# Eight instead of six buffers for the q and k chunks of a fused attention and star-ReLU kernel

## The chip, the cores and the metric

The kernel runs on one core of one Trainium2 chip. The metric is the device time of one execution in microseconds (us), the median of several. TensorE is called PE below (PEld is its weight load), VectorE DVE, ScalarE ACT, GpSimd POOL, SyncE SP. "L566" is line 566 of the program; in experiments that add lines the same statement has a number up to eight higher.

## The reference, cut to what matters

```python
def _attn_ref(q, k, v, tau):                 # each (4, 6080, 256), float32
    qn = q / (np.linalg.norm(q, axis=1, keepdims=True) + 1e-06)
    kn = k / (np.linalg.norm(k, axis=1, keepdims=True) + 1e-06)
    s = kn.transpose(0, 2, 1) @ qn / tau     # 256 x 256 for each batch
    a = softmax(s)                           # cut: max, exp, sum
    return v @ a

def _moe_ref(x, w_in, w_out, s, b):          # x: 24320 x 256, w_in: 256 x 2048
    r = np.maximum(x @ w_in, 0.0)
    return (s * (r * r) + b) @ w_out
```

For each of the four batches the kernel needs the whole of q and k, summed into one 256 x 256 matrix (the "Gram" matrix), before it can start on that batch's rows. It does so for a batch while PE works on the rows of the one before. Only the first batch has nothing to hide behind.

## The kernel before

q and k arrive in chunks of 512 rows (13 chunks for the first batch, 12 for each later one). One buffer holds one chunk of both in fp16, 4 KiB a partition. The four fp32 pieces of w_out have the same size and take buffers of the same pool.

```python
    qk_pool = pool("qk_pool", 6)
    # ... (cut)
        def load(self, c):
            at, np_, jc = self.chunks[c]
            t = qk_pool.tile([P, 2, JC, C], FP16, tag="qk", name="qk")
            # ... (cut: the first two chunks of batch 0 take another way)
                    po(nc.gpsimd.dma_start(out=t[:np_, i, :jc, :], in_=rows))
    # ... (cut) after the first batch's chunks:
    for i in range(NPIECE):                                     # 4 pieces
        w32 = qk_pool.tile([P, 4, C], FP32, tag="qk", name="w32")
        po(nc.gpsimd.dma_start(out=w32, in_=w_out_rows[:, ts(i, 4), :]))
        w_pieces.append(w32)
```

`po` keeps the instructions of an engine in program order. So POOL issues the loads of q, k and v one after the other, and a load whose buffer isn't free holds up all behind it. A tile's buffer is chosen when the program is built: a free one, or the one that is given back next.

The work of the later batches is spread over numbered program steps. What matters here is the second batch (batch 1): chunk c is loaded 16 steps ahead of its use, its four pairs of Gram matmuls (L142) follow, and its squares for the norms come on ACT (k) and DVE (q, L162):

```python
            for j in range(JC):
                at_step(w0 + span * (c * JC + j) / n, lambda gr=gr, c=c, j=j: gr.mm(c, j))

            def norm_step(gr=gr, c=c, sc=sc):
                ops = gr.norm_ops(c)          # square of k, square of q, two folds
                for i, f in enumerate(ops):
                    at_step(int(sc) + 2 + 1 + i * 3, f)
```

The pieces of w_out are read by casts and sums at steps 7 to 44; the last reader of piece 1 comes at step 38 (L470), of piece 4 at step 44. The third chunk is asked for at step 24.

## Time and profile before

| | before |
|---|---|
| median of the first three runs | 730.93 us (729.64 to 731.26) |
| span of the profiled run | 727.9 us (its time: 729.62 us) |
| PE busy, first 40 us | 25.58 us |
| PE busy, 76 to 721 us | 644.39 of 645 us |
| waits of PE from 40 to 722 us | 3.2 us, of them 2.0 in one piece |

The table says that PE is the bound from 40 us on, and that reading the first batch is a stage of its own, limited by the transfers. The rows that carry it are in the prediction.

### The profile page before, as it was taken

Reading aid. Unit: us, or ns where it says so; the run is one execution under the profiler, and the core shown is the slowest. Engines: PE = TensorE matmul, PEld = TensorE weight load, DVE = VectorE, ACT = ScalarE, POOL = GpSimd, SP = SyncE. Lnnn points to the kernel's source line nnn. Section 1 sums busy time; section 2 is a strip of 40 time slices with the busy share of each in tenths; the row PEclk is TensorE's granted clock in tenths of the full one; section 3 lists DMA queues with packets and bytes.
Section 4 is the critical chain, followed back from the end, with each engine's and each line's share of the span. In section 5 each row is a group of like instructions: output and inputs, shape, how many; then the busy total and the mean of one; then the engine's idle time right before and its main releaser. Section 6 shows DMA issues by size and latency. Waiting matters only on the chain.

```text
span 727.9 us, 17843 instructions
## 1 busy us (share of the span) xinstructions
PE 705.5 (97%) x7618; PEld 509.7 (70%) x7618; DVE 623.9 (86%) x873; ACT 541.6 (74%) x582; POOL 82.4 (11%) x158
## 2 busy tenths in 40 slices
PE   4799899999999999999999999999999999999997
PEld 3556677776777777777677777777668777777776
DVE  4779899988888989898788989998888888888886
ACT  4489777787777777788777777778777777777872
POOL 4520420001121110001110210000000000000000
PEclk9999999999999999999999999999999999999999
DMA  9995995236497654333767585323333333321201
GB/s 235 209 258 69 209 207 109 61 88 128 92 142 161 128 96 99 88 73 66 141 124 137 119 145 130 71 62 72 84 74 77 88 75 73 96 59 47 78 30 74
DMA packets 81600, 79.57 MB, mean 109 GB/s; under 512 B 55696, under 2 KB 56528, under 8 KB 81520
## 3 DMA queue, kind: packets, MB, share of 16 engines
q0 software_dynamic: 21472, 39.46, 31.9%
q1 hardware_dynamic: 59616, 37.64, 19.9%
q8 instruction: 60, 0.98, 0.6%
q10 hardware_dynamic: 432, 1.31, 0.5%
q14 instruction: 20, 0.16, 0.1%
HBM read 78.91 MB, written 24.90 MB: 143 GB/s over the span
## 4 chain that ended last, share of the span: by engine, by line
PE 89%; DMA 5%; ACT 3%; DVE 2%; issue 1%; POOL 0%; ACTq 0%; POOLq 0%; DVEq 0%
PE h_ps L566 43%; PE o_ps L710 38%; PE s_ps L142 4%; DMA qk<-in_q_dram 3%; PE wa_ps L278 2%; ACT r L576 1%; DMA raw<-in_q_dram 1%; PE o_ps L614 1%; ACT g L587 1%; ACT sq L165 0%; ACT L222 0%; DVE f L178 0%; PE t_ps L241 0%; DVE o_sb L594 0%; DVE S L638 0%
## 5 line engine op out<-in xcount | busy, mean ns | idle before, releaser
L576 ACT ACTIVATE r<-h_ps 128x1024 f16<-128x1024 f32 (+1 forms) x384 | 387.8, 1013 | 154.3 <-PE h_ps L566 152.7
L566 PE MATMUL h_ps<-vT,wa 128*128 128x512 f16 (+7 forms) x1632 | 451.9, 364 | 0.6 <-ACT r L576 0.4
L710 PEld LDWEIGHTS <-S 128*128 128x128 f16 x2944 | 198.1, 98 | 86.3 <-issue 1.5
L710 PEld LDWEIGHTS <-g 128*128 128x128 f16 x2208 | 155.0, 98 | 74.1
L589 DVE TENSOR_TENSOR g<-r 128x2048 f16<-128x2048 f16 (+2 forms) x154 | 176.3, 1145 | 17.7 <-ACT r L576 17.3
L710 PE MATMUL o_ps<-T,S 128*128 128x128 f16 x2208 | 183.7, 219 | 0.9 <-ACT nrm L222 0.4
L566 PEld LDWEIGHTS <-wa 128*128 128x128 f16 x1632 | 136.2, 98 | 21.6 <-issue 1.0
L710 PE MATMUL o_ps<-w_out,g 128*128 128x128 f16 x1472 | 134.2, 219 | 0.0
L594 DVE SCALAR_TENSOR_TENSOR o_sb<-o_ps,s_out,u 128x256 f32<-128x256 f32 x138 | 66.4, 481 | 52.8 <-PE o_ps L710 50.8
L587 ACT ACTIVATE g<-r 128x1024 f16<-128x1024 f16 x93 | 97.9, 1053 | 0.0
L142 PE MATMUL s_ps<-qk 128*128 128x256 f16 (+1 forms) x384 | 70.6, 285 | 15.6 <-ACT qk L133 7.0
L325 POOL DMA_DIRECT2D v<-in_v_dram x48 | 25.7, 536 | 506.3 <-DMA vT<-v 346.4
L594 DVE SCALAR_TENSOR_TENSOR u<-o_ps,s_out,rowconst 128x256 f32<-128x256 f32 x138 | 65.9, 478 | 3.6 <-PE o_ps L710 2.4
L710 PE MATMUL o_ps<-w_out,S 128*128 128x128 f16 x736 | 63.4, 219 | 0.0
L710 PE MATMUL o_ps<-N,g 128*128 128x128 f16 x736 | 63.4, 219 | 0.0
L165 ACT ACTIVATE sq<-qk 128x1024 f16<-128x1024 f16 (+3 forms) x49 | 50.4, 1033 | 10.7 <-DMA qk<-in_k_dram 7.5
L638 DVE TENSOR_TENSOR S<-S,g 128x2048 f16<-128x2048 f16 (+1 forms) x47 | 56.4, 1201 | 1.3
L636 DVE TENSOR_TENSOR S<-g 128x2048 f16<-128x2048 f16 (+1 forms) x47 | 56.0, 1192 | 0.0
L642 DVE TENSOR_TENSOR S<-g,S 128x2048 f16<-128x2048 f16 x46 | 55.9, 1215 | 0.0
L640 DVE TENSOR_TENSOR S<-g 128x2048 f16<-128x2048 f16 x46 | 55.8, 1214 | 0.0
L142 PEld LDWEIGHTS <-qk 128*128 128x128 f16 (+1 forms) x384 | 33.1, 102 | 21.7 <-DVE qk L132 9.1
L162 DVE TENSOR_TENSOR sq<-qk 128x1024 f16<-128x1024 f16 (+3 forms) x49 | 33.0, 673 | 2.8 <-DMA qk<-in_q_dram 2.8
(68 smaller groups left out, 281.6 us busy)
## 6 DMA issues: line engine op xcount, KB each, us to landing
out_dram<-o_sb SPq DMA_DIRECT2D x46, 512.0 KB, 3.0
v<-in_v_dram POOLq DMA_DIRECT2D x47, 256.0 KB, 3.9
qk<-in_k_dram POOLq DMA_DIRECT2D x42, 256.0 KB, 6.8
qk<-in_q_dram POOLq DMA_DIRECT2D x42, 256.0 KB, 7.6
vT<-v SPq DMA_TRANSPOSE x182, 2.8
w<-in_moe_w_out_dram POOLq DMA_DIRECT2D x4, 512.0 KB, 12.0
raw<-in_q_dram ACTq DMA_DIRECT2D x2, 512.0 KB, 6.6
raw<-in_k_dram SPq DMA_DIRECT2D x2, 512.0 KB, 7.0
```

What stands on the lines that cost most here:

```text
L142: po(nc.tensor.matmul(self.s_ps[:, ch, :], kc[:np_, j, ts(ch, P)], qc[:np_, j, :], start=(c == 0 and j == 0 and ch == 0), stop=(c == len(s ...
L165: po(nc.scalar.activation(out=st["sq"][:np_, 1, js, :], in_=kc[:np_, js, :], func=AF.Square))
L566: po(nc.tensor.matmul(dst, wa[:, ci, ts(m, P)], src, start=(ci == 0), stop=(ci == CH - 1), skip_group_check=True))
L576: po(nc.scalar.activation(out=r16[:, :, i % 2, :n], in_=h_tiles.pop((g, i))[:, :, :n], func=AF.Relu))
L587: po(nc.scalar.activation(out=dst, in_=src, func=AF.Square))
L589: po(nc.vector.tensor_mul(dst, src, src))
L594: po(nc.vector.scalar_tensor_tensor(out=dst, in0=src, scalar=s_out, op0=ALU.mult, in1=add, op1=ALU.add))
L636: po(nc.vector.tensor_add(T[1], A21, A22))
L638: po(nc.vector.tensor_sub(T[2], T[1], A11))
L640: po(nc.vector.tensor_sub(T[3], A11, A21))
L642: po(nc.vector.tensor_sub(T[4], A12, T[2]))
L710: po(nc.tensor.matmul(st[name][:, j, :], a()[:, i, ts(j, P)], w[:, i, :], start=first, stop=last, skip_group_check=True))
```

## The change

It is to keep the second batch's first chunks from waiting for buffers that hold w_out.

```diff
-    qk_pool = pool("qk_pool", 6)
+    qk_pool = pool("qk_pool", 8)
```

No instruction is added, removed or moved: the programs of the two kernels are the same on every engine, but for addresses and waits.

## The prediction

> **What bounds the kernel now.** I read the page first, then the table of waits for TensorE (PE) alone, then the order of work on GpSimd and PE around the one wait that matters, then DMA use in 2 us steps.
>
> ```profile
> span 727.9 us, 17843 instructions
> PE 705.5 (97%) x7618; PEld 509.7 (70%) x7618; DVE 623.9 (86%) x873; ACT 541.6 (74%) x582; POOL 82.4 (11%) x158
> PE 89%; DMA 5%; ACT 3%; DVE 2%; issue 1%; POOL 0%; ACTq 0%; POOLq 0%; DVEq 0%
> ```
>
> PE is busy for 97% of the span and holds 89% of the chain that ended last. So a buffer can be worth only the time in which PE stands still for it. Busy time of PE by stretches gives where it stands: 25.58 of the first 40.00 us (the first batch's q and k are being read), 32.16 of 40 to 73, 1.00 of 73 to 76, 644.39 of 645 from 76 to 721, 2.36 of the last 6.9. Between 40 and 722 us the table of PE's waits is, in full:
>
> ```profile
> PE s_ps L142 <- DMA qk<-in_q_dram: 2.0, 1, 2.0
> PE h_ps L566 <- ACT r L576: 0.4, 1, 0.4
> PE o_ps L710 <- ACT nrm L222: 0.4, 2, 0.2
> PE o_ps L710 <- DVE S L636: 0.2, 1, 0.2
> PE o_ps L710 <- ACT T L470: 0.2, 1, 0.2
> ```
>
> One wait of 2.0 us for a chunk of q stands out; the others sum to 1.2 us. Which chunk? From the order of work on PE, the Gram matmuls (L142) of the second batch come in pairs from 60.33 us on; four pairs are chunk 1, four more (66.84 to 71.59) are chunk 2, and the pair at 75.88, after the wait, opens the third chunk. On GpSimd, which issues these loads (start, duration, engine, line, what; in brackets the idle time before and what ended it):
>
> ```profile
> 59.31 0.53 POOL L325 DMA_DIRECT2D v<-in_v_dram  x1 [9.52 <-DMA vT<-v]
> 68.58 0.53 POOL L126 DMA_DIRECT2D qk<-in_k_dram  x1 [8.74 <-PE h_ps L566]
> 69.10 0.54 POOL L126 DMA_DIRECT2D qk<-in_q_dram  x1
> 74.00 0.53 POOL L126 DMA_DIRECT2D qk<-in_k_dram  x1 [4.37 <-ACT T L470]
> 74.52 0.54 POOL L126 DMA_DIRECT2D qk<-in_q_dram  x1
> 75.04 0.55 POOL L325 DMA_DIRECT2D v<-in_v_dram  x1
> ```
>
> Chunk 3 is issued at 68.58 after 8.74 us of waiting, chunk 4 at 74.00 after 4.37 more. All six buffers are taken: four by the fp32 pieces of w_out (read by DVE and ACT up to the cast of 80.45 us, L470), two by chunks 1 and 2. Chunk 4's releaser is named plainly: a cast of a piece, L470. Chunk 3's is named a PE matmul, but L566 does not read this pool; DVE's square of chunk 1 (L162, 67.28 + 0.68 = 67.96 us) ends beside it, and I take chunk 1's buffer for the one handed on. Either way it is a buffer that is missing. Then the chain of waits, start and length:
>
> ```profile
> 68.58 0.43 POOL qk L126
> 69.01 0.09 issue
> 69.10 6.74 DMA qk<-in_q_dram
> 75.83 0.04 issue
> 75.88 0.38 PE s_ps L142 x2
> ```
>
> The load is issued at 69.10, takes 6.74 us to land, and PE goes on 0.05 us later. What lies before it is the point:
>
> ```profile
> 64.00:66.00 2.00, 2.00 (x15) 1.31 (x14) 1.09 (x2) 1.58 (x2) 0.00 (x0) 1.00 0.00 0
> 66.00:68.00 2.00, 2.00 (x16) 1.32 (x14) 1.86 (x3) 1.72 (x4) 0.00 (x0) 1.00 0.00 0
> ```
>
> The last two columns are DMA share and GB/s: for 4 us no transfer runs at all, while GpSimd waits for a buffer.
>
> **What the Trainium skill says.** "DMA: Bandwidth & Descriptors", section "Anatomy of one DMA — SWDGE (gpsimd) path": DMA engines do not wait on semaphores; any wait is on the issuing sequencer, before dispatch. The trace agrees: the wait sits on GpSimd, nothing moves, and the v load behind chunk 4 goes out at 75.04, at once after it. The same page, section "SWDGE vs HWDGE vs iDMA": a DMA that casts can only be issued from GpSimd. The program agrees: q and k go from fp32 to fp16, and these loads and v's share that one in-order queue. "Perfetto Trace Analysis", section "Optimization Strategy": the same gap repeating on the engine that should be saturated can mean that there is no SBUF for the next tile. Here the gap on PE occurs once, not repeatedly, which bounds the gain. "SBUF — State Buffer", section "SBUF size: 192, 224, or 256?": about 208 KiB a partition are usable; no view of the profile shows the room. Two more buffers are 2 x 2 x 4 x 256 x 2 bytes = 8 KiB a partition; adding up the pools of the program I get roughly 180 KiB before, an estimate, so it should fit.
>
> **The change part by part.** It removes and adds no instruction and no byte. It adds two buffers.
>
> First batch, 0 to 40 us: eight loads (four chunks) go out from 1.60 to 5.38 us, the ninth at 11.81 after 5.83 us of waiting for a square (L165). With eight buffers it need not wait for that buffer. But the DMA share is 1.03 to 1.14 in every 2 us step from 4 to 30 us, and the rate holds at 204 to 212 GB/s from 10 to 30 us. The engines always have work queued, so an earlier issue lengthens the queue and lands nothing sooner: the last piece of q lands at 34.57 either way. I book 0.0 us.
>
> Second batch: with eight, four buffers hold pieces and four are free, so chunks 1 to 4 wait for none. Chunks 1 and 2 already land in time. Chunk 3 can go right after the v load at 59.31, at 59.31 + 0.53 = 59.84 us (that load's own wait, on transposes of v, stays), its q half at about 60.4. Allow it the 6.74 us it took before: it lands by 67.1. PE asks for it when its matmul (73.32 + 0.55) is done, 73.87. So it is early by 6.8 us, and the wait of 75.88 - 73.87 = 2.01 us goes. Chunk 4 goes at about 60.9 instead of 74.00. Chunk 5 then meets the pieces, but is issued once chunk 1's buffer is free (67.96), against 75.66 before, while PE needs it some 14 program steps after chunk 3, at about 1 us each: hidden.
>
> Does another engine pay the 2 us back? ACT works without a pause from 68.34 to 75.23 and, before the change, stood idle for 1.55 us because PE stood. Shifted by 2 us, the relu of the pair of products held up would be wanted at about 74.7 and starts when ACT is free, 75.13 to 75.23: 0.5 us late. Two h_ps buffers take that up: PE's next pair, wanted at 77.13 - 2.01 = 75.12, needs the relu that ends at 73.91 + 1.03 = 74.94, 0.18 us to spare. The last cast of T3 (80.45 before) would end about 78.85, PE wants it at 80.75 - 2.01 = 78.74: a 0.1 us wait, as the 0.15 us there now. DVE finishes its product (L589) at 75.05 + 1.22 = 76.27, its next eviction (77.06 before) starts 0.8 us earlier, and it has caught up by 82, where it had waits of 0.34 and 0.89 us. Sum: 2.0 us removed, 0 to 0.3 handed back.
>
> From 76 us on PE is busy 644.39 of 645 us whatever the loads do, so everything moves forward by 2 us and nothing else changes. 730.93 - 2.0 = **728.9 us**.
>
> **The rivals.** (a) A different wait takes the place: ACT or DVE, filled between 66 and 76 us, hold PE by the margins just named (0.18 us for the relu). For it: ACT busy 2.00 of 2.00 from 70 to 74. Against: PE waits for ACT in no place there now except 0.15 us. It would leave 1 us or less of the gain: about 730. (b) The start gets shorter too, because deeper queueing smooths 16 DMA engines: PE stands still for 14.4 us of the first 40, and 4.8 of it waiting on q. Against: saturated DMA at a constant rate. It could give another 0.5 to 1 us: 728. (c) The loads, now earlier, collide with something: chunks 3 and 4 at 60 to 68 us meet the stretch that is empty now, and chunk 5 at 68.5 takes chunk 3's old place beside an output store (69.31) and four transposes of v (69.79). That is the load of before, so no new collision; a loss would need v's transposes late by tens of us. (d) The buffer was not what chunk 3 waited for, since the named releaser is a PE matmul. Then the 2 us stay: 730.9.
>
> **Range and chances.** The sum says -2.0; (a) and (d) pull towards 0, (b) to -3. The three runs of before span 1.6 us (729.64 to 731.26), about as much as the effect. So 727.4 to 730.6. 2% would be 14.6 us, and PE stands still for 22.4 us in the whole span, most of it in the first 40 us, which is DMA-bound: faster by over 2% is 1%, slower 1%, within 2% is 98%.
>
> **What would show it.** Right: no wait for a q chunk in PE's table between 40 and 722 us; chunk 3 issued near 59.8, chunk 4 near 60.9; DMA traffic between 60 and 68; the first-batch q still landing near 34.6. Wrong: the pair of Gram matmuls that opens chunk 3 still waits; PE waits on ACT or DVE near 75 us by a microsecond or more; or the first 40 us become shorter or longer by over 0.5 us.

## The result, and the profile after

| | before | after |
|---|---|---|
| median | 731.1 us (4 runs, 729.64 to 731.6) | 727.42 us (4 runs, 727.38 to 727.61) |
| ratio | 1 | 0.9954 (95% interval 0.9936 to 0.9971) |
| span of the profiled run | 727.9 us | 725.6 us |

A ratio is the mean time of one kernel's fast runs over that of the other's in the same rounds, so not quite the ratio of the medians. The gain is 3.7 us at the median, 2.2 us between the two profiled runs (729.62 and 727.38), and the spread of the runs shrank from 2 us to 0.23.

The page of the kernel after, the lines that answer to those of before:

```profile
span 725.6 us, 17836 instructions
PE 704.5 (97%) x7618; PEld 509.2 (70%) x7618; DVE 623.6 (86%) x873; ACT 541.5 (75%) x582; POOL 82.4 (11%) x158
PE 89%; ACT 4%; DMA 4%; DVE 1%; issue 1%; ACTq 0%; DVEq 0%; POOLq 0%
```

All waits of PE between 40 and 722 us after:

```profile
PE h_ps L566 <- ACT r L576: 0.4, 1, 0.4
PE o_ps L710 <- ACT nrm L222: 0.4, 2, 0.2
PE o_ps L710 <- DVE S L636: 0.2, 1, 0.2
PE o_ps L710 <- ACT T L470: 0.2, 1, 0.2
```

It is the list of before without its first line, the 2.0 us for a chunk of q. POOL's order of work after (start, duration, engine, line, what, and in brackets the idle time before it):

```profile
59.18 0.53 POOL L325 DMA_DIRECT2D v<-in_v_dram  x1 [9.50 <-DVE acc L438]
59.70 0.54 POOL L126 DMA_DIRECT2D qk<-in_k_dram  x1
60.22 0.55 POOL L126 DMA_DIRECT2D qk<-in_q_dram  x1
60.74 0.56 POOL L126 DMA_DIRECT2D qk<-in_k_dram  x1
61.26 0.57 POOL L126 DMA_DIRECT2D qk<-in_q_dram  x1
61.78 0.58 POOL L325 DMA_DIRECT2D v<-in_v_dram  x1
68.50 0.53 POOL L126 DMA_DIRECT2D qk<-in_k_dram  x1 [6.14 <-PE h_ps L566]
```

The third and the fourth chunk now go out without a gap behind the load of v at 59.18. The 8.7 us wait has become one of 6.14 and has moved to the fifth chunk, which PE wants much later. The stretch in which nothing moved before is full (the last two columns are DMA share and GB/s):

```profile
64.00:66.00 2.00, 2.00 (x14) 1.29 (x14) 1.00 (x2) 1.58 (x3) 0.00 (x0) 1.00 1.08 195
66.00:68.00 2.00, 2.00 (x15) 1.27 (x13) 1.96 (x3) 1.62 (x4) 0.00 (x0) 1.00 1.11 203
```

So the mechanism is as predicted. But a wait of 2.0 us doesn't explain 3.7 us at the median, nor why the runs now agree so closely. The experiments went after that.

### The profile page after: what moved, and what is told of

Its sections match the earlier page's. It is cut to its first block, busy times and chain, and to the rows that moved or that the text cites. A ratio compares the mean times of both kernels' runs of the same rounds, so it can differ in the third digit from the quotient of the medians.

```text
span 725.6 us, 17836 instructions
## 1 busy us (share of the span) xinstructions
PE 704.5 (97%) x7618; PEld 509.2 (70%) x7618; DVE 623.6 (86%) x873; ACT 541.5 (75%) x582; POOL 82.4 (11%) x158
## 4 chain that ended last, share of the span: by engine, by line
PE 89%; ACT 4%; DMA 4%; DVE 1%; issue 1%; ACTq 0%; DVEq 0%; POOLq 0%
PE h_ps L566 43%; PE o_ps L710 38%; PE s_ps L142 4%; DMA qk<-in_q_dram 2%; PE wa_ps L278 2%; ACT r L576 2%; DMA raw<-in_q_dram 1%; PE o_ps L614 1%; ACT g L587 1%; ACT sq L165 1%; DVE f L178 0%; ACT L222 0%; PE t_ps L241 0%; ACT T L470 0%; DVE o_sb L594 0%
## 5 line engine op out<-in xcount | busy, mean ns | idle before, releaser
L566 PE MATMUL h_ps<-vT,wa 128*128 128x512 f16 (+7 forms) x1632 | 451.9, 364 | 0.6 <-ACT r L576 0.4
L566 PEld LDWEIGHTS <-wa 128*128 128x128 f16 x1632 | 136.1, 98 | 21.6 <-issue 1.0
L162 DVE TENSOR_TENSOR sq<-qk 128x1024 f16<-128x1024 f16 (+3 forms) x49 | 33.0, 673 | 2.8 <-DMA qk<-in_q_dram 2.8
```

The lines of the kernel that those rows point to most:

```text
L566: po(nc.tensor.matmul(dst, wa[:, ci, ts(m, P)], src, start=(ci == 0), stop=(ci == CH - 1), skip_group_check=True))
```

## The experiments

Three theories for the rest of the gain. **A**: in most runs of before the wait is longer than in the profiled one. **B**: the first batch gains too. **C** came up after the first runs: the pause does something to PE beyond the time that it lasts.

### The kernel before, traced again

Run unchanged, for a second trace.

> The kernel before, unchanged, for a second trace. Its four times so far spread over 2 us (729.64 to 731.6), those of the changed kernel over 0.23 us. Theory A (the spread of before is the length of the one wait for the third chunk, which then is longer than the traced 2.0 us in most runs): a trace of a run near 731 shows PE waiting some 3.0 to 3.5 us for that chunk and everything else as in the first trace. Rival B (the rest of the gain, 1.3 us, comes from the first batch): a wait of 2.0 us again, and the last piece of q of the first batch landing over 1 us later than 34.4 us.

It took 731.42 us. The record marks every run here fast or unknown; "slow" in this text means the upper of the two groups into which the times of the unchanged kernel fall, 730.9 us and above. This is a slow run, and neither A nor B showed: the wait was 2.1 us against 2.0, and the two traces differ little up to the wait. What differs comes after it. A row for 76 to 80 us, first of the profiled fast run, then of this one; after the POOL column stand the granted clock of PE, the DMA share and GB/s:

```profile
76.00:80.00 4.00, 4.00 (x43) 2.92 (x42) 2.81 (x5) 2.73 (x4) 2.32 (x5) 1.00 1.21 137
```

```profile
76.00:80.00 4.00, 4.00 (x24) 2.65 (x24) 2.39 (x4) 1.32 (x2) 2.22 (x5) 0.57 1.28 130
```

PE is busy for all 4 us in both, but it begins 43 matmuls in one and 24 in the other, because the clock that it was granted is 0.57 of full speed. Busy time alone hides this. Cut into single microseconds the clock reads 0.62, 0.50, 0.50, 0.67 and then 1.00 again. The order of work on PE shows when the change came, a fraction of a microsecond after work resumed:

```profile
75.91 0.38 PE L142 MATMUL s_ps<-qk 128*128 128x256 f16 x2 [2.13 <-DMA qk<-in_q_dram]
76.12 0.93 PE L566 MATMUL h_ps<-vT,wa 128*128 128x512 f16 x2
76.85 0.84 PE L710 MATMUL o_ps<-T,S 128*128 128x128 f16 x6
...
79.62 0.62 PE L566 MATMUL h_ps<-vT,wa 128*128 128x512 f16 x2
80.08 0.55 PE L710 MATMUL o_ps<-w_out,g 128*128 128x128 f16 x7
```

The first pair (0.38 us) runs at full speed; the pair of 128x512 after it takes 0.93 us, against 0.59 at full clock. From 79.62 on it is nearly, from 80.08 fully as before. What it cost: 4 us at 0.57 are 4 x 0.43 = 1.7 us of full-speed work, and this run is 731.42 - 729.62 = 1.8 us behind the fast one. That is theory C: the pause not only lasts 2 us, in some runs it also costs PE its clock for some 3.4 us afterwards.

The Trainium skill knows such a thing. "TensorE: Matmul & The Clock Gate", section "What's actually happening", says that PE's clock is halved after a window of about 3.4 us without work and restored after about as long with work, and that the window runs free of the program, so that it is a matter of the run where it falls. The trace agrees on the half clock (0.50) and the length of the recovery (3.4 us). It doesn't agree on a whole window without work: a pause of 2.1 us sufficed. Whether the traces show the window is asked below, when there are more of them.

### Each half of the change alone

Six buffers as before, and two of their own for the two chunks:

```diff
+    qk2_pool = pool("qk2_pool", 2)
...
-            t = qk_pool.tile([P, 2, JC, C], FP16, tag="qk", name="qk")
+            if self.b == 1 and c in (2, 3):
+                t = qk2_pool.tile([P, 2, JC, C], FP16, tag="qk2", name="qk")
+            else:
+                t = qk_pool.tile([P, 2, JC, C], FP16, tag="qk", name="qk")
```

> Six buffers as before, and two of their own for the third and fourth chunk of the second batch: the second batch's part of the change alone. Theory A: the whole gain, 727.4 us (727.1 to 727.8), no wait for q between 40 and 722 us. Rival B: only the traced 2.0 us, 728.7 to 729.2.

Measured: 727.49 us (5 runs, 727.37 to 727.86), ratio 0.9956. The second batch's half is the whole gain.

Eight buffers, two of them held until step 44 (one element set by DVE after the first batch, read again at step 44):

```diff
-    qk_pool = pool("qk_pool", 6)
+    qk_pool = pool("qk_pool", 8)
...
+    held = [qk_pool.tile([P, 4, C], FP32, tag="qk", name="held") for _ in range(2)]
...
```

> Eight buffers, but two of them held from the end of the first batch until program step 44, so that the second batch has as few as before: the first batch's part alone. Theory A: as before, 729.6 to 731.6, with the wait of 2 us or more for the third chunk still there, although the ninth load goes out near 10.1 us instead of 11.8. Rival B: 1.3 us faster, near 729.6 at the median.

Measured: 729.82 us (6 runs: five from 729.73 to 730.04, one of 731.5), ratio 0.9991 (0.9978 to 1.0004). Its ninth load went out at 9.92 us, against 11.81 before, and it gained nothing by it. The wait for the third chunk is still there:

```profile
PE s_ps L142 <- DMA qk<-in_q_dram: 2.2, 1, 2.2
```

Its median lies at the fast end of before, but its runs form the same two clusters. One slow run of six against about half in before is too few to call a difference (if half are slow, one or none of six comes by chance in 11% of such trials), and no run is faster than before's fastest (729.41). With the first experiment this puts the whole gain on the second batch, and B falls.

### Whose buffer the third chunk waited for

The profile named a PE matmul of L566 as the releaser, which doesn't read this pool; the prediction took DVE's square of the first chunk (L162) instead. Six buffers, with only that square moved three steps ahead:

```diff
+                    early = 3 if gr.b == 1 and c == 0 and i == 1 else 0
-                    at_step(int(sc) + 2 + 1 + i * 3, f)
+                    at_step(int(sc) + 2 + 1 + i * 3 - early, f)
```

> Six buffers; only DVE's square of the second batch's first chunk is placed three program steps earlier. If that square is the last reader of the buffer that the third chunk waits for (my reading), the load goes out near 65.5 us instead of 68.58, lands by 72.5, and the PE wait at 73.9 is gone: 727.4 us (727.1 to 728.3), with no buffer added. If the named releaser (a PE matmul of L566 at 67.87) is the real one, the load still goes out at 68.5 and the time stays at 729.6 to 731.6.

Measured: 727.76 us (5 runs, 727.39 to 727.83), ratio 0.9957. POOL's line for the third chunk:

```profile
66.08 0.53 POOL L126 DMA_DIRECT2D qk<-in_k_dram  x1 [6.21 <-DVE rowconst L443]
```

DVE's line for the square, first of before, then of this run:

```profile
67.28 0.68 DVE L162 TENSOR_TENSOR sq<-qk 128x1024 f16<-128x1024 f16 x1
```

```profile
64.78 0.69 DVE L162 TENSOR_TENSOR sq<-qk 128x1024 f16<-128x1024 f16 x1
```

The square ran at 64.78 instead of 67.28 us, the load went out 2.5 us earlier (at 66.08; 65.5 was expected), and no wait for q is left in PE's table (ACT's at the h_ps line is 0.2 us longer, DVE's of 0.2 us is gone). So the square was the last reader of the buffer, and the named releaser was only the event nearest in time, as it is here again with L443. Moving one 0.68 us instruction is worth within 0.4 us as much as two buffers.

### The wait without the pause

To tell theory C from all that counts time: the wait stays, but PE does something in it. Nine matmuls that nobody reads go ahead of the third chunk's first pair (the body of `keep_warm` is cut).

```diff
+                if b == 1 and c == 2 and j == 0:
+                    at_step(w0 + span * (c * JC + j) / n, keep_warm)   # 9 matmuls of 128x512
                 at_step(w0 + span * (c * JC + j) / n, lambda gr=gr, c=c, j=j: gr.mm(c, j))
```

> The kernel before with nine matmuls of 128x512 whose result nobody reads, put on PE just ahead of the third chunk's first Gram matmul: some 1.94 us of work (9 x 0.216) inside the 2.0 us wait. The wait for the chunk stays, only PE's standing still goes. Theory C (formed from the second trace of before, where the granted clock is 0.50 from about 76.4 to 79.7 us after a wait of 2.1 us: the lost rest of the gain is PE at half clock after the pause, in some runs and not in others): all runs at the fast end of before, 729.4 to 730.1, spread below 0.7 us, and PEclk 1.00 from 73 to 80 us. Rival A (the wait itself is longer in the slow runs) or B (the first batch): the spread of before stays, 729.4 to 732, median 731.

Measured: 729.84 us, all five runs from 729.58 to 729.98, while the nine runs of before beside them went from 729.61 to 731.98 (five of them above 731). The trace:

```profile
73.92 2.11 PE L476 MATMUL idle_ps<-w_in 128*128 128x512 f16 x9
76.22 0.38 PE L142 MATMUL s_ps<-qk 128*128 128x256 f16 x2 [0.19 <-DMA qk<-in_q_dram]
```

The chunk arrives no earlier (76.22), so nothing of the wait is won back. But PE stands still for only 0.19 us, the clock is 1.00 from 76 to 80 us, and the slow runs are gone (if half were still slow, five fast ones in a row would come once in 32 trials). This is C, and A falls with it.

### More traces of before, and a shorter pause

> The kernel before, unchanged, a third trace. Theory C: if the run is near 729.6 to 730.0, PEclk is 1.00 throughout 73 to 80 us; if it is near 731.4, PEclk is about 0.5 for some 3 us after the wait; the wait itself is 2.0 to 2.2 us either way. Rival A: the wait differs by over 1 us between the two kinds of run.

> The kernel before once more, for the tie between time and clock, which so far rests on one slow trace (731.42, clock 0.50 for some 3 us) and two fast ones (729.62 and 729.55, clock 1.00). Theory C: above 730.9 us, a stretch at a clock of about 0.5 between 76 and 80 us; below 730.1, a clock of 1.00 there. Against it: a slow run with full clock, or a fast one with half.

> As the fourth: above 730.9 us, a stretch at a clock of about 0.5 between 76 and 80 us; below 730.1, a clock of 1.00 there.

They took 729.55, 729.72 and 729.87 us. All three have a wait of 2.0 to 2.1 us and a clock of 1.00 from 76 to 80 us. So four fast traces have full clock and one slow trace half clock; no trace contradicts C, but the slow side rests on a single one, since no other slow run was caught with a trace. The length of the wait doesn't decide: 2.1 us occur on both sides.

Its place does, as far as these traces go. Each trace keeps the instants at which the granted clock changed, and they lie on a grid: every stretch between two changes is a whole number of steps of 3.413 us (in the slow trace 18, 1 and 190 of them; with five buffers, below, 16, 3, 2, 2 and 190; in each fast trace a single stretch of 208 or 209, up to the drop after PE's last work). In the slow trace the whole pause (73.78 to 75.91 us) falls into one step, and at the end of that step the clock drops, for just one step. Row by row, a step each:

```profile
72.83:76.25 3.42, 1.29 (x15) 0.89 (x13) 3.35 (x5) 2.30 (x5) 2.27 (x5) 1.00 1.24 244
76.25:79.66 3.41, 3.41 (x22) 2.27 (x20) 1.93 (x3) 1.32 (x2) 1.97 (x4) 0.50 1.31 125
79.66:83.07 3.41, 3.26 (x34) 2.27 (x33) 1.98 (x4) 2.79 (x4) 1.30 (x3) 1.00 1.08 200
```

In the four fast traces of before and in that of the first batch's half alone, the end of a step cuts the pause, and its larger part is 1.17 to 2.01 us. The closest case is the fifth trace (steps counted back from its drop at 726.04 us):

```profile
74.09:77.50 3.41, 1.40 (x14) 1.07 (x14) 2.48 (x5) 1.72 (x4) 3.33 (x7) 1.00 1.24 210
77.50:80.91 3.41, 3.41 (x38) 2.43 (x36) 3.00 (x5) 2.92 (x5) 0.90 (x2) 1.00 1.32 92
```

So the clock fell where PE stood still for 2.13 us of one step, and stayed where it was at most 2.01. The end of the program, after PE's last matmul, bears it out in all the runs: where 1.81 to 1.92 us of the step were left (three traces), the clock stayed to the end of the next step; where 2.29 to 3.28 us were left (eight), it fell at the end of that very step. No step in the thirteen traces goes against a limit between 2.01 and 2.13 us. An estimate from these numbers: a pause of 2.1 us lies whole within a step in (3.413 - 2.1) / 3.413 = 38% of all positions, and 16 of 33 timed runs were slow (48%). That a slow run is one in which the pause crosses this limit still rests on one slow trace.

With four unread matmuls instead of nine:

> Four unread matmuls instead of nine inside the same wait: PE stands still for about 1.1 us instead of 2.0. Theory C, if it is the length of the pause that counts: fewer or no runs at half clock, all or nearly all of 729.4 to 730.2. If any pause there is enough to lose the clock: a spread as before, half of the runs above 730.9.

729.63 us, five runs from 729.57 to 730.09, with a pause of 1.1 us, which in the traced run lies whole within one step (73.51 to 76.92 us) without a drop of the clock. As expected if the length counts, but the runs of before beside it were mostly fast as well (two of nine above 730.9), so the times alone don't show that 1.1 us are safe; the steps with up to 2.01 us of standing still at full clock speak for it.

The timed runs of before are 33: 15 lie below 730.2 us, 2 at 730.4, 16 from 730.9 to 732.04. That is what the medians of about 731 consist of.

### More and fewer buffers

> Seven buffers: three are free of pieces when the second batch starts, so the third chunk goes out near 59.8 us as with eight, and the fourth at 68.5 (when the first chunk's buffer comes free), landing by 76 while PE wants it at about 79. Theory: the whole gain, 727.4 us (727.1 to 727.9), no wait for q, one buffer saved. Rival: the fourth chunk needs a buffer too; a wait on PE near 79 us and a time above 728.3.

Seven: 727.46 us (4 runs, 727.4 to 727.6), ratio 0.9953, no wait for q. The fourth chunk waited for the first one's buffer, until 68.50 us, and still came in time. The eighth buffer does nothing for the time.

> Five buffers: the second chunk of the second batch has to wait for the first one's buffer (68.5 us) while PE wants it at 66.8, so it lands near 75.5; the third chunk waits for a piece and lands some 6 us after PE wants it. Theory: two waits of about 8 and 4 us on PE, each followed by some us at half clock: 731 + 11 + 0 to 4 = 742 to 746. Rival (buffers matter only for the third and fourth chunk): below 735.

Five: 746.1 us (4 runs, 745.74 to 746.4), ratio 1.0207 (1.0193 to 1.0222), at the upper end of the 742 to 746 expected. PE's wait for q between 40 and 722 us, and a row for 76 to 80 us, after the first of the two pauses:

```profile
PE s_ps L142 <- DMA qk<-in_q_dram: 13.9, 2, 8.9
```

```profile
76.00:80.00 4.00, 3.91 (x17) 2.17 (x17) 0.00 (x0) 1.16 (x2) 0.00 (x0) 0.50 0.65 75
```

The pauses last 8.9 and 5.0 us, and here the clock falls within the pause, in the first already at about 71.3 us. PE then works at half clock from 76.09 to about 81.5 and from 90.15 to about 95.2 us, some 10.4 us that count half: an estimate of 5.2 us lost. With 13.9 of waiting that makes 19.1, against 746.1 - 727.5 = 18.6 measured over seven buffers. In this run a pause of several microseconds cost its length plus some 2.5 us.

No experiment pointed to a version clearly faster than the changed kernel. Seven buffers run level with it and take 4 KiB a partition less; the early square runs within 0.4 us of it and takes none.

## Why the prediction was right or wrong

The measured 727.42 us lies just inside the range (727.4 to 730.6), 1.5 us below the predicted 728.9; "within 2%" is what came. That the range holds it, by 0.02 us, is luck: its lower end was set for the spread and for rival (b), a gain in the first batch, and neither is where the rest of the gain came from.

- **The wait for the third chunk goes: right.** Chunks 3 and 4 were predicted near 59.8 and 60.9 us and went out at 59.70 and 60.74. The wait of 2.01 us is gone from PE's table.
- **The missing buffer was the first chunk's, held by DVE's square: right,** against the profile's own label. The early square showed it; rival (d) falls.
- **Nothing from the first batch: right.** The ninth load went out at 10.09 us, held up now by a landing instead of a buffer. The last piece of q landed at 34.32 us (34.57 before), but the matmuls on it begin at 34.36 us, and at 34.31 to 34.61 in the five traces of the unchanged kernel, and the first batch's half alone was not faster than before's fast runs. Rival (b) falls.
- **0 to 0.3 us handed back by ACT and DVE: right.** Their waits on PE are the same as before to a tenth. Rival (a) falls, and so does (c): no new wait on v.
- **The step that failed is the sum, "730.93 - 2.0".** The term of 2.0 us is sound for a run that keeps its clock: 729.62 - 727.38 = 2.2. Of the 0.2 on top, 0.16 is the way in which the wait was counted, from the modelled end of the matmuls before it (73.87 us), though unhindered the next pair starts before such an end (after the change at 73.62, where theirs is 73.23 + 0.55 = 73.78); and the run after was 0.1 us ahead before the wait (its last pair of the second chunk at 71.49 against 71.59). But it came from the fastest run's trace and was taken off a median that other runs make. In about half of the runs the pause also halved PE's clock for some 3 us, 1.8 us more, and that went with it. So the term is 2.2 us in one half of the runs and some 4 in the other.
- **"About as much as the effect", said of the spread of 1.6 us, was the missed clue.** I took the spread for noise that widens the range. It was an effect of the very pause under study, and it went when the pause went (0.23 us).

What decides in a run whether the clock falls is not the length of the wait within 2.0 to 2.2 us, but how much of it falls into one step of the 3.413 us grid, which runs free of the program as the Trainium skill has it (the end of a step lies at 72.83 us in the slow trace and at 73.98 to 74.78 in four fast ones). The limit lies between 2.01 and 2.13 us of one step. Missing is a second trace of a slow run.

## What to carry to other kernels

Before taking a wait's length from a trace, look where the traced run lies among the timed ones; if the bound engine is PE and the times form two clusters, trace a run of each and compare the granted clock after every pause of 2 us or more. Here a pause of PE of 2 us cost up to 4, which makes even a single one of 2 us worth removing, or filling with unread matmuls if it can't be removed. And before adding buffers, find the last reader of the one that is missing: here an instruction moved three steps did the same.

## What the Trainium skill lacked or had wrong

- "TensorE: Matmul & The Clock Gate", section "Why this matters for your kernels", warns of PE-idle gaps of over about 3 us. Here a gap of 2.1 us was followed by a clock of 0.50 (one trace, 731.42 us), while gaps of 2.0 to 2.2 us left it at 1.00 in five other traces. What parts them is the length inside one step of 3.413 us: 2.13 us and more of it lost the clock, at most 2.01 kept it, in all thirteen traces. With a gap of 1.1 us no slow run occurred in five.
- The same page has nothing on telling such runs from the times alone. Here they are the upper of two clusters 1.8 us apart, 16 of 33 runs, and vanish when unread matmuls fill the gap (5 of 5 runs within 0.4 us).
- "Perfetto Trace Analysis", section "Optimization Strategy", ties missing buffers to a gap that repeats. Here the gap came once in 728 us and was a missing buffer all the same.
- No page says that the releaser that a profile names for a buffer can be a bystander: L566 before, L443 with the early square, where the last reader was L162 (ends at 67.96 and 65.47 us).
